# Decay rows of the first head pair: spread on chip by TensorE and ScalarE instead of loaded by DMA

## The chip, the cores and the metric

The kernel runs on one core of a Trainium2 chip. The metric is the device time of one execution in microseconds (us), the median of the runs shown. Engines are named as the profile names them: PE (TensorE), DVE (VectorE), ACT (ScalarE), POOL (GpSimd) and SP (SyncE, which here only issues DMAs).

## What is computed

Three stages follow one another: an attention with a decay, a mixture of experts with one expert for each token, and a dense feed-forward layer. Only the start of the attention matters here:

```
scores = scale * np.matmul(q, k.transpose(0, 1, 3, 2))
log_f = np.log(np.clip(f, 0.0001, 1.0))
cum = np.cumsum(log_f, axis=-1)
decay = cum[:, :, :, None] - cum[:, :, None, :]
scores = np.where(causal, -1000000000.0, scores + decay)
```

After this come a softmax over the last axis and the product with `v`. There are 4 x 8 = 32 heads, 576 positions and a head dimension of 64. The part of the decay that is constant along a row of the scores falls out of the softmax, so the kernel needs only one row of `cum` for each head, and the same row in every partition.

## The kernel before, in words

The function `attention` works on 16 pairs of heads. A pair has five blocks of query rows, u = 0 to 4, taken in the order 3, 0, 1, 4, 2. Block u < 4 covers 128 rows and 128(u+1) columns for each of the two heads; block 4 covers the last 64 rows of both heads at once and all 576 columns. The list `seq` holds the 80 (pair, block) steps and the loop from line 590 walks through them with lags: in one turn it computes the scores of a step, the softmax of the same step, and the transposes, products with v, normalisations and so on of earlier steps. Every engine takes its instructions in the order in which the program emits them; nothing is reordered by a scheduler. A helper tagged "T" owns three PSUM banks that are reused in turn: transposed q and k, the tails, the transposed probabilities and small results all pass through these three. Tag "s" gives three banks to the scores.

The decay goes as follows. `fs` (32 heads in 32 partitions, 576 columns) is loaded, clipped (L172), its logarithm taken (L174), summed up by a scan (L178) and multiplied by -8 (L179), which gives `cum`, again 32 x 576 in float32. The ScalarE queue stores it to the DRAM tile `ncum` (L564). `load(i, "c")` then fetches for pair i a tile `cb` of 128 x 3 x 576: `cb[:, 0]` and `cb[:, 1]` hold the row of head 0 and of head 1 in all partitions, `cb[:, 2]` holds head 0 in partitions 0 to 63 and head 1 in 64 to 127 (L162, L163; four DMAs for a pair, all on SP's queue). The softmax of blocks 0 to 3 reads at most 512 columns of `cb[:, h]` (L311); block 4 reads `cb[:, 2]` in two halves of 288 (L322). The result of L311 is the row maximum `mx`, which the exponential on ACT (L314) needs.

The start, before the loop, in emission order:

- SP: loads of q, k and v of pair 0 and q of pair 1 (L149, L150); then `cb` of pair 0, then k, v and `cb` of pair 1.
- PE: transposes of q and k of pair 0 (`prep(0, 0)`, `prep(0, 1)`, L212) and of their last 64 rows (`prep(0, 2)`, L228).
- ACT and DVE: the transposed values are split into a rounded part in type F32R (`hi`, ACT) and a remainder (`lo`, DVE, L219); a score is the sum of three products hi·hi, hi·lo and lo·hi (L289).
- ACT then squares v of pair 0 (L254), squares the expert embeddings (L577), loads a table, takes a square root (L578), and loads the first table again (L579).
- DVE converts a number of constants (L710 to L713).

In the first turn of the loop (step (0, 3)) PE computes the scores, ACT takes the exponentials of head 0, PE transposes q of pair 1 (`prep(1, 0)`), ACT copies them to `qraw` (L221), POOL splits `qraw` (L222, L223), and ACT takes the exponentials of head 1. At the end of that turn the second half of `scale(0)` runs (a small matmul `vb`, L259, bits of it on DVE, L261, factors on POOL, L264 to L270), and then `vprep(0)` scales and splits v on POOL (L245 to L247). The next turn brings `prep(1, 1)`, the same for k of pair 1 (L212, `kraw` L221, L222, L223), and two turns later POOL makes `vmb` (L256), which the matmul `vb` of pair 1 (L259) reads; behind that matmul PE has the tails of pair 1 (L228) and the first products with v (L412).

Of the kernel before, what the change touches and what calls it, by code (L numbers as in the profile page):

```python
# [9 lines left out]
F32 = mybir.dt.float32  # L10
# [5 lines left out]
ACTF = mybir.ActivationFunctionType  # L16
# [8 lines left out]
B, H, S, D = 4, 8, 576, 64  # L25
# [6 lines left out]
T = 5 * B  # L32
# [24 lines left out]
def body(ctx, tc, q, k, v, f, emb, tau, w1, w2, win, wout, out):  # L57
# [38 lines left out]
    with ExitStack() as acc:  # L96
        ps_s = attention(tc, g, acc, q, k, v, f, emb, tau, w1)
        g.home = ctx.enter_context(tc.tile_pool(name="home", bufs=16, reuse_waits="tile"))
        ring = ctx.enter_context(tc.tile_pool(name="ring", bufs=8, reuse_waits="tile"))

        def wtile(dt=F32R, n=1024):
            return (ring.tile([128, n], dt, name="wh", tag="wh"), ring.tile([128, n], dt, name="wl", tag="wl"))

        g.wtile = wtile
        g.w2a = w2[0]
        with ExitStack() as rtx:
            route(tc, g, rtx.enter_context(tc.tile_pool(name="r_p", bufs=1)), ps_s)
# [12 lines left out]
def attention(tc, g, acc, q, k, v, f, emb, tau, w1):  # L120
    nc = tc.nc
    ident, xd, ncum, nrm = g.ident, g.xd, g.ncum, g.nrm
    with ExitStack() as ctx:
        cst = ctx.enter_context(tc.tile_pool(name="a_cst", bufs=1))
        ld = ctx.enter_context(tc.tile_pool(name="a_ld", bufs=3))
# [4 lines left out]
        ps_t = acc.enter_context(tc.tile_pool(name="a_pt", bufs=3, space=PSUM))  # L130
# [13 lines left out]
        loaded = {}  # L144

        def rows_in(t, src, i):
            b, h0 = i // 4, 2 * (i % 4)
            for h in range(2):
                nc.sync.dma_start(t[:, 0:4, h], src[b, h0 + h, 0:512, :].rearrange("(k p) d -> p k d", p=128))  # L149
            nc.sync.dma_start(t[0:64, 4], src[b, h0:h0 + 2, 512:S, :].rearrange("h p d -> p h d"))  # L150
            return t

        def load(i, what):
            r = loaded.setdefault(i, {})
            for nm in what:
                if nm == "v":
                    r[nm] = rows_in(vbuf[i % 3], v, i)
                elif nm == "c":
                    bh = 2 * i
                    c = r[nm] = ld.tile([128, 3, S], F32, name="cb", tag="cb")  # L160
                    for h in range(2):
                        nc.sync.dma_start(c[:, h], ncum[bh + h:bh + h + 1, :].to_broadcast([128, S]))  # L162
                        nc.sync.dma_start(c[64 * h:64 * h + 64, 2], ncum[bh + h:bh + h + 1, :].to_broadcast([64, S]))  # L163
                else:
                    r[nm] = rows_in(ld.tile([128, 5, 2, D], F32, name=nm + "t", tag=nm + "t"), q if nm == "q" else k, i)

        load(0, "qkv")
        load(1, "q")

        zer = cst.tile([128, 128], F32, name="zer")  # L170
        nc.vector.memset(zer, 0.0)
        nc.vector.tensor_scalar(fs, fs, 1e-4, 1.0, op0=ALU.max, op1=ALU.min)  # L172
        lf = cst.tile([B * H, S], F32, name="lf")
        nc.scalar.activation(lf, fs, ACTF.Ln)  # L174
# [2 lines left out]
        cum = cst.tile([B * H, S], F32, name="cum")  # L177
# [23 lines left out]
        consts = route_consts(tc, g, cst)  # L201
        next(consts)
        split = {}

        def prep(i, part):
            r = loaded[i]
# [33 lines left out]
        def vprep(i):  # L240
            r = loaded[i]
            vf, vp = r["v"], vpart[i % 3]
            vs = qk.tile([128, 5, 2, D], F32, name="vs", tag="vs", bufs=1)
            v1, v2 = vp[:, :, :, 0:D], vp[:, :, :, D + 2:2 * D + 2]
            nc.gpsimd.tensor_scalar(vs, vf, vscale[i], 0.0, op0=ALU.mult, op1=ALU.add)  # L245
            nc.gpsimd.tensor_scalar(v1, vs, 1.0, 0.0, op0=ALU.mult, op1=ALU.add)
            nc.gpsimd.tensor_sub(v2, vs, v1)  # L247
            r["vp"] = vp
# [315 lines left out]
        nc.scalar.dma_start(ncum, cum)  # L564
        prep(0, 1)
        prep(0, 2)
        load(0, "c")
        load(1, "kvc")
        vs0 = scale(0)
        next(vs0)  # L570
# [19 lines left out]
        for n in range(n_all + Lg + 1):  # L590
# [38 lines left out]
            for x in (pt_, sf):  # L629
                for _ in x:  # L630
                    pass
            if n == 0:
                for _ in vs0:
                    pass
                vprep(0)
# [1079 lines left out]
```

## Time and profile before

| | us |
|---|---|
| median of 3 runs | 892.55 |
| lowest, highest | 892.10, 892.96 |
| the profiled execution, its own time | 891.38 |
| its span, first to last instruction | 889.6 |

| engine | busy us | share of the span |
|---|---|---|
| PE | 855.0 | 96% |
| DVE | 699.5 | 79% |
| ACT | 564.4 | 63% |
| POOL | 377.1 | 42% |

A timeline row gives the start, the duration, the engine, the line, the operation, what it writes and reads with its shape, a count where equal instructions are merged (then the duration is that of all of them), and in brackets the idle time of the engine before it with what ended that time. The end of a row is its start plus its duration. PE's ends are modelled. A wait that hung on several things is put down to the one that came last by the profile. Queue names end in q (SPq: SP issuing a DMA).

### The profile page before, as it was taken

Reading aid. Unit: us, or ns where it says so; the run is one execution under the profiler, and the core shown is the slowest. Engines: PE = TensorE matmul, PEld = TensorE weight load, DVE = VectorE, ACT = ScalarE, POOL = GpSimd, SP = SyncE. Lnnn points to the kernel's source line nnn. Section 1 sums busy time; section 2 is a strip of 40 time slices with the busy share of each in tenths; the row PEclk is TensorE's granted clock in tenths of the full one; section 3 lists DMA queues with packets and bytes.
Section 4 is the critical chain, followed back from the end, with each engine's and each line's share of the span. In section 5 each row is a group of like instructions: output and inputs, shape, how many; then the busy total and the mean of one; then the engine's idle time right before and its main releaser. Section 6 shows DMA issues by size and latency. Waiting matters only on the chain.

```text
span 889.6 us, 17326 instructions
## 1 busy us (share of the span) xinstructions
PE 855.0 (96%) x6308; PEld 594.8 (67%) x6308; DVE 699.5 (79%) x1542; ACT 564.4 (63%) x1052; POOL 377.1 (42%) x517
## 2 busy tenths in 40 slices
PE   5999999999759999999999999999999999999998
PEld 4788787887658999998889744444444445664443
DVE  4888888888879677787789778878878778777875
ACT  5778879788564566665856766655555444666453
POOL 6678677777142322422604233344223322435221
PEclk9999999999879999999999999999999999999999
DMA  7978566682336977878668110002000100100001
GB/s 173 195 162 170 136 153 157 143 235 58 109 113 244 319 281 271 273 261 287 229 222 299 37 50 13 25 13 72 25 1 36 37 1 1 60 1 25 1 1 47
DMA packets 102830, 109.73 MB, mean 123 GB/s; under 512 B 62964, under 2 KB 72200, under 8 KB 102736
## 3 DMA queue, kind: packets, MB, share of 16 engines
q1 hardware_dynamic: 97266, 93.49, 36.3%
q0 software_dynamic: 5184, 14.87, 4.7%
q8 instruction: 51, 0.84, 0.4%
q14 instruction: 43, 0.35, 0.1%
q10 hardware_dynamic: 286, 0.17, 0.1%
HBM read 93.31 MB, written 15.20 MB: 122 GB/s over the span
## 4 chain that ended last, share of the span: by engine, by line
PE 62%; DVE 5%; POOL 2%; issue 1%; ACT 1%; DMA 0%; DVEq 0%; POOLq 0%
PE h L1580 18%; PE y L1626 14%; PE y L1188 12%; PE h L1208 11%; PE t L1626 5%; POOL e L1594 1%; DVE r L1591 1%; DVE e L1605 1%; PE t L1110 1%; PE t L1441 1%; PE h L1278 1%; DVE wl L1057 1%; DVE e L1606 0%; DVE u L1593 0%; DMA xg<-xd,gidx 0%
## 5 line engine op out<-in xcount | busy, mean ns | idle before, releaser
L1594 POOL TENSOR_TENSOR e<-u,e 128x512 f32<-128x512 f32 (+1 forms) x80 | 105.0, 1313 | 238.8 <-DVE u L1593 235.5
L1590 ACT ACTIVATE e<-h,s_h 128x512 f32<-128x512 f32 (+1 forms) x80 | 51.2, 640 | 114.9 <-PE h L1580 114.9
L1626 PE MATMUL y<-dw,gh 128*128 128x512 f16 x448 | 113.6, 379 | 0.2 <-ACT ob L1634 0.2
L1612 DVE SCALAR_TENSOR_TENSOR gl<-e,s_gup,gh 128x512 f16<-128x512 f32 (+1 forms) x80 | 94.7, 1183 | 8.4 <-ACT gh L1610 7.9
L1626 PEld LDWEIGHTS <-gh 128*128 128x128 f16 x576 | 56.3, 98 | 64.8 <-issue 0.5
L340 DVE SCALAR_TENSOR_TENSOR pts<-pt,pts 128x512 f16<-128x512 f32 (+3 forms) x128 | 69.8, 567 | 12.8 <-ACT pts L337 12.0
L1208 PE MATMUL h<-xh,wh 128*128 128x384 f32 (+1 forms) x256 | 79.2, 309 | 0.6 <-DVE hl L1214 0.4
L1208 PE MATMUL h<-xl,wh 128*128 128x384 f32 (+1 forms) x256 | 79.0, 309 | 0.6 <-DVE xl L1112 0.6
L1591 DVE TENSOR_SCALAR r<-h,s_h 128x512 f32<-128x512 f32 (+1 forms) x80 | 55.6, 695 | 30.5 <-ACT e L1590 30.5
L1208 PE MATMUL h<-xh,wl 128*128 128x384 f32 (+1 forms) x256 | 78.8, 308 | 0.0
L1580 PEld LDWEIGHTS <-wh 128*128 128x128 f16 x480 | 46.9, 98 | 46.7 <-issue 0.3
L1580 PEld LDWEIGHTS <-wl 128*128 128x128 f16 x480 | 47.0, 98 | 46.4
L1610 ACT ACTIVATE gh<-e,s_gup 128x512 f16<-128x512 f32 (+1 forms) x80 | 53.7, 671 | 36.1 <-DVE e L1606 36.1
L337 ACT ACTIVATE pts<-pt 128x512 f16<-128x512 f32 (+3 forms) x128 | 58.5, 495 | 22.6 <-PE pt L360 11.0
L314 ACT ACTIVATE p<-sm,mx 128x512 f32<-128x512 f32 (+3 forms) x128 | 67.9, 558 | 1.7 <-DVE mx L311 1.5
L1188 PE MATMUL y<-wh,hh 128*128 128x512 f32 x168 | 67.7, 403 | 0.0
L1605 DVE TENSOR_TENSOR e<-r,e 128x512 f32<-128x512 f32 (+1 forms) x80 | 50.4, 630 | 21.3 <-POOL e L1594 21.3
L311 DVE CUSTOM_DVE_ANT_0 sm<-s,cb 128x512 f32<-128x512 f32 (+3 forms) x128 | 58.3, 484 | 11.0 <-PE s L291 6.5
L1188 PE MATMUL y<-wl,hh 128*128 128x512 f32 x168 | 65.7, 391 | 0.0
L1626 PE MATMUL y<-dw,gl 128*128 128x512 f16 x224 | 65.3, 379 | 0.0
L1580 PE MATMUL h<-yth,wh 128*128 128x512 f16 x192 | 64.9, 379 | 0.0
L1580 PE MATMUL h<-yth,wl 128*128 128x512 f16 x192 | 64.9, 379 | 0.0
(368 smaller groups left out, 2436.4 us busy)
## 6 DMA issues: line engine op xcount, KB each, us to landing
raw<-in_moe_w_dram SPq DMA_DIRECT2D x44, 512.0 KB, 4.9
spare<-in_moe_w_dram SPq DMA_DIRECT2D x24, 512.0 KB, 5.7
cb<-ncum SPq DMA_DIRECT2D x32, 288.0 KB, 4.9
raw<-in_moe_w_in_dram SPq DMA_DIRECT2D x16, 512.0 KB, 4.9
raw<-in_moe_w_out_dram SPq DMA_DIRECT2D x16, 512.0 KB, 4.5
yg<-yd SPq DMA_DIRECT2D x18, 264.0 KB, 2.7
cb<-ncum SPq DMA_DIRECT2D x32, 144.0 KB, 4.8
qt<-in_q_dram SPq DMA_DIRECT2D x32, 128.0 KB, 2.8
```

Of the source, the lines that this page charges most:

```text
L311: nc.vector.tensor_tensor_reduce(out=s[:, 0:n], in0=ps[h][:, 0:n], in1=c[:, h, 0:n], scale=-0.125, scalar=1e30, op0=ALU.add, op1=ALU.min, ...
L314: nc.scalar.activation(p[:, 0:n], s[:, 0:n], ACTF.Exp, scale=-1.0, bias=m)
L337: nc.scalar.activation(hi, ps, ACTF.Copy, scale=UP)
L340: nc.vector.scalar_tensor_tensor(lo, ps, UP, hi, op0=ALU.mult, op1=ALU.subtract)
L1188: nc.tensor.matmul(py[a], x[:, 128 * a:128 * a + 128], w[:, fb % 2], start=(fb == 0 and m == 0 and w is wh), stop=(fb == 7 and m == 1))
L1208: nc.tensor.matmul(pl, x[:, fs], y[:, c], start=(c == 0 and m == 0), stop=(c == 3 and m == 2))
L1580: nc.tensor.matmul(pl, w[:, fs], x[:, d], start=(d == 0 and m == 0), stop=(d == 3 and m == 2))
L1591: nc.vector.tensor_scalar(r, pl, back, 0.0, op0=ALU.mult, op1=ALU.max)
L1594: nc.gpsimd.tensor_sub(e, u, e)
L1605: nc.vector.tensor_sub(d, r, d)
L1612: nc.vector.scalar_tensor_tensor(gl, d, s, gh, op0=ALU.mult, op1=ALU.subtract)
L1626: nc.tensor.matmul(PO[c][a], x, w, start=(fb == 0 and m == 0 and w is wh), stop=(fb == FB - 1 and m == 1))
```

## The change

The three rows of `cb` of pair 0 are no longer loaded. Four columns of the identity are spread into `pickrow`, a 32 x 3 x 128 tile of zeros and ones in float32. `decay(j)` multiplies the picker j with 512 columns of `cum`, both float32, into a PSUM bank of tag "T", and ACT copies the bank into `cb[:, j]`. For j = 2 the remaining 64 columns follow as a second matmul and copy. `decay(0)` and `decay(1)` are emitted right after `prep(0, 2)`, ahead of the loads of k, v and `cb` of pair 1 and of `scale(0)`; `decay(2)` is emitted at the end of the first turn of the loop, ahead of the second half of `scale(0)`. All other pairs load 512 instead of 576 columns into `cb[:, 0]` and `cb[:, 1]`. `ncum` is still stored.

```
                     for h in range(2):
-                        nc.sync.dma_start(c[:, h], ncum[bh + h:bh + h + 1, :].to_broadcast([128, S]))
+                        nc.sync.dma_start(c[:, h, 0:512], ncum[bh + h:bh + h + 1, 0:512].to_broadcast([128, 512]))
                         nc.sync.dma_start(c[64 * h:64 * h + 64, 2], ncum[bh + h:bh + h + 1, :].to_broadcast([64, S]))
...
         nc.vector.memset(zer, 0.0)
+        pickrow = cst.tile([B * H, 3, 128], F32, name="pickrow")
+        for j, (x, y, h) in enumerate(((0, 128, 0), (0, 128, 1), (0, 64, 0), (64, 128, 1))):
+            nc.vector.tensor_copy(pickrow[:, min(j, 2), x:y], ident[0:B * H, h:h + 1].to_broadcast([B * H, y - x]))
...
+        def decay(j):
+            c = loaded[0]["c"]
+            for lo, hi in ((0, 512), (512, S)) if j == 2 else ((0, 512),):
+                t = ps_t.tile([128, 512], F32, name="dec", tag="T")
+                nc.tensor.matmul(t[:, 0:hi - lo], pickrow[:, j], cum[:, lo:hi], start=True, stop=True)
+                nc.scalar.activation(c[:, j, lo:hi], t[:, 0:hi - lo], ACTF.Copy)
...
         prep(0, 2)
-        load(0, "c")
+        loaded[0]["c"] = ld.tile([128, 3, S], F32, name="cb", tag="cb")
+        decay(0)
+        decay(1)
         load(1, "kvc")
         vs0 = scale(0)
...
             if n == 0:
+                decay(2)
                 for _ in vs0:
```

## Rows read from the trace of the kernel before

**Rows 1.** Busy time by stretch: engines PE, PEld, DVE, ACT, POOL, granted clock, DMA share, GB/s

```profile
0.00:20.00 20.00, 10.58 (x48) 7.19 (x49) 9.45 (x41) 10.73 (x19) 12.32 (x55) 1.00 0.74 171
40.00:60.00 20.00, 20.00 (x277) 16.66 (x275) 16.58 (x63) 17.08 (x40) 16.66 (x24) 1.00 0.71 160
```

**Rows 2.** Waits, first 20 us: who waited for whom, total us, times, longest

```profile
POOL qhi L222 <- ACT qraw L221: 4.8, 1, 4.8
...
DVE sm L311 <- DMA cb<-ncum: 3.6, 2, 2.1
```

**Rows 3.** Waits of PE from 40 to 240 us, the longest total

```profile
PE s L289 <- DVE mx L322: 1.4, 3, 0.5
```

**Rows 4.** Timeline of ACT

```profile
8.91 0.23 ACT L231 ACTIVATE khi<-tail 128x64 fp32r<-128x64 f32 x1 [0.99 <-DVE qlo L232]
9.05 0.74 ACT L254 ACTIVATE vs<-vb 128x640 f32<-128x640 f32 x1
...
12.02 1.28 ACT L579 ACT_TABLE_LOAD   x1
13.82 0.72 ACT L314 ACTIVATE p<-sm,mx 128x512 f32<-128x512 f32 x1 [0.51 <-DVE mx L311]
14.45 0.58 ACT L221 ACTIVATE qraw<-tps 128x512 f32<-128x512 f32 x1
15.97 1.01 ACT L314 ACTIVATE p<-sm,mx 128x512 f32<-128x512 f32 x2 [0.94 <-DVE mx L311]
18.02 0.60 ACT L221 ACTIVATE kraw<-tps 128x512 f32<-128x512 f32 x1 [1.04 <-PE tps L212]
...
23.52 0.23 ACT L231 ACTIVATE qhi<-tail 128x64 fp32r<-128x64 f32 x1
...
24.99 0.78 ACT L328 ACTIVATE p<-sm,mx 128x576 f32<-128x576 f32 x1 [0.73 <-DVE mx L322]
...
31.88 0.74 ACT L254 ACTIVATE vs<-vb 128x640 f32<-128x640 f32 x1 [0.86 <-DMA vb<-in_v_dram]
```

**Rows 5.** Timeline of POOL

```profile
15.11 0.62 POOL L222 TENSOR_SCALAR qhi<-qraw 128x512 fp32r<-128x512 f32 x1 [4.80 <-ACT qraw L221]
...
21.56 1.28 POOL L223 TENSOR_TENSOR klo<-kraw,khi 128x512 fp32r<-128x512 f32 x1
22.81 0.19 POOL L256 TENSOR_SCALAR vmb<-vm 128x1 bf16<-128x1 f32 x1
```

**Rows 6.** Timeline of PE

```profile
4.47 1.09 PE L212 MATMUL tps<-ident,qt 128*128 128x128 f32 x4 [4.47 <-DMA qt<-in_q_dram]
...
7.86 0.79 PE L289 MATMUL s<-khi,qhi 64*128 64x512 f32 x2 [0.28 <-ACT khi L218]
...
9.95 0.40 PE L291 MATMUL s<-maskb,identb 128*128 128x128 bf16 x2
...
16.90 1.09 PE L212 MATMUL tps<-ident,kt 128*128 128x128 f32 x4 [1.83 <-DMA kt<-in_k_dram]
...
22.29 0.44 PE L350 MATMUL pt<-ident,p 128*128 128x128 f32 x2
23.05 0.16 PE L259 MATMUL vb<-vmb,onesb 128*128 128x1 bf16 x1 [0.32 <-DMA qt<-in_q_dram]
```

**Rows 7.** Line 212 over the whole span: duration ns min/median/max, first and last start us

```profile
L212 PE MATMUL tps<-ident,qt x64: 272/273/447, 4.5 to 206.8; 128*128 128x128 f32 x64
```

**Rows 8.** The chain that ended last, one piece: start, us, what (F32R matmuls, 512 columns)

```profile
282.91 12.29 PE y L1188 x54
```

**Rows 9.** Timeline of DVE

```profile
3.56 0.47 DVE L172 TENSOR_SCALAR fs<-fs 32x576 f32<-32x576 f32 x1 [2.55 <-DMA fs<-in_f_dram]
...
7.45 0.69 DVE L219 TENSOR_TENSOR qlo<-tps,qhi 128x512 fp32r<-128x512 f32 x1
8.06 0.68 DVE L219 TENSOR_TENSOR klo<-tps,khi 128x512 fp32r<-128x512 f32 x1
...
13.09 0.69 DVE L311 CUSTOM_DVE_ANT_0 sm<-s,cb 128x512 f32<-128x512 f32 x1 [2.14 <-DMA cb<-ncum]
```

**Rows 10.** Timeline of SP's queue

```profile
8.97 0.35 SPq L162 DMA_DIRECT2D cb<-ncum  x1
...
11.03 1.14 SPq L149 DMA_DIRECT2D kt<-in_k_dram  x2
```

## The prediction

> **What bounds the kernel now.** I read the stretches first, then the waits, then each engine's timeline up to 35 us. From 40 us on PE is busy in all of a 20 us stretch, in the first 20 us in little over half [rows 1]; from 40 to 240 us the longest total wait of PE is 1.4 us, and it is for DVE [rows 3]. So this kernel is a start of some 23 us that fills slowly and then one long stretch that PE paces. The change acts on the start alone, and a shift of the moment at which PE gets going is carried to the end one for one.
>
> In the start DVE waits 3.6 us for `cb` of pair 0 [rows 2]. That is the wait that the change removes, and it looks like the bound. It is not: the first softmax step on DVE runs at 13.09 us [rows 9] and ACT's exponential follows at 13.82, but ACT has its own queue before it. It goes without a break from the square of v at 9.05 to the end of the second table load at 12.02 + 1.28 = 13.30 us [rows 4]. With `cb` there at once, the exponential could move from 13.82 to 13.30: the wait is worth 0.52 us at most.
>
> What ends last in the start is read backwards from PE's matmul `vb` of pair 1 at 23.05 [rows 6]. The profile names a DMA for that wait, but the matmul reads `vmb`, which POOL finishes at 22.81 + 0.19 = 23.00 [rows 5]. POOL has been at work since 15.11 with gaps of some tenths at most: it splits q of pair 1, makes the factors, scales and splits v, splits k (ends at 22.84), makes `vmb` [rows 5]. At 15.11 it had waited 4.80 us for `qraw`, which ACT ended at 14.45 + 0.58 = 15.03 behind that first exponential [rows 2, 4, 5]. Behind `vb` stand PE's tails of pair 1, then ACT at 23.52 and, through DVE, the exponential at 24.99 [rows 4]. So the chain is: ACT's queue to 13.30, exponential, `qraw`, POOL to 23.00, `vb`, all the rest. **Whatever is put into ACT's queue ahead of the first exponential, beyond those 0.52 us, is paid at the end.**
>
> **The change part by part.**
>
> Pickers on DVE: four copies of 32 partitions and up to 128 columns. No row has the shape; four times 0.47 (32 x 576, wider) makes 1.9 us at most, four times nothing at least. DVE idles 2.55 us before L172 [rows 9], so they cost nothing; without that cover they would delay `cum`, which is done well before its reader, PE at 8.19 (next).
>
> The two matmuls on PE. Their banks are the fourth and fifth of tag "T", which has three: the first takes over that of q and waits for DVE's qlo, to 7.45 + 0.69 = 8.14; the second that of k, to 8.06 + 0.68 = 8.74 [rows 9]. With 0.05 for the release (`vmb` to `vb` above) PE starts at 8.19. Before, it had started the scores at 7.86 [rows 6]; these now stand behind both matmuls.
>
> The length of such a matmul is not in the trace: no float32 product that isn't a transpose exists. Bounds from the nearest rows. Below, one pass of F32R: 12.29 / 54 = 0.228 us for 512 columns late in the kernel [rows 8]. [...] Between, the float32 transposes: four take 1.09 us and one takes 0.447, so each adds (1.09 - 0.447) / 3 = 0.214 for 128 columns [rows 6, 7], 0.86 for 512, two passes. Above, four passes: 4 x 0.43 = 1.71. I take **1.71**. [...] A modelled 0.23 (0.447 - 0.214) follows until the result is there. So the first runs from 8.19 and is there at 10.13, the second from 9.90, there at 11.84.
>
> [...]
>
> The two copies on ACT: 0.60 each, as `kraw` [rows 4]. They stand behind khi, which ends at 8.91 + 0.23 = 9.14, and ahead of the square of v. The second can start at 11.84 and ends at 12.44. Everything behind it shifts by 12.44 - 9.14 = 3.30, so ACT is through at 16.60 instead of 13.30, and the exponential goes from 13.82 to 16.60: **+2.78**. Its maximum is ready: the scores took 7.86 to 10.35 [rows 6], so from 11.61 they end by 14.1, and L311 takes 0.69. Queued behind ACT's wait are `qraw` (17.81) and with it POOL's row, `vmb` (25.78) and `vb` (25.83).
>
> With two passes the matmuls are there at 9.28 and 10.13, the second copy ends at 10.73, the shift is 1.59, the exponential +1.07. With one pass ACT takes the copies back to back, 9.14 to 10.3, and the exponential is +0.6 late.
>
> `decay(2)`: 512 and 64 columns, 1.9 us of PE and some 0.8 of ACT. PE has that time, waiting for `qraw` in any case: `vb` of pair 0 now gets the bank of q of pair 1. ACT's two copies come behind the second exponential, about 18.4 to 19.2. The transposes of k of pair 1 need the first copy's bank, so they go from 16.90 to about 19.0, 2.1 late; PE's work up to 22.73 [rows 6] then ends by 24.8, inside the wait for `vb` at 25.83. Nothing is added, by 1 us.
>
> Loads: SP's four issues from 8.97 to 11.03 go [rows 10], so k, v and `cb` of pair 1 are issued about 2.8 us earlier, and PE's wait of 1.83 for k at 16.90 [rows 6] vanishes. It lay beside POOL's chain; zero. The later wait of ACT for v at 31.88, 0.86 [rows 4], goes too; behind it ACT next waited for PE, so I count nothing. The 64 columns less per load: no PE wait in the long stretch is for a DMA worth naming; zero. On both I allow a gain of 0.5.
>
> The sum is +2.78 against the profiled 891.38, that is 894.2; the median of the runs lies 1.17 higher, so 892.55 + 2.78 = **895.3 us**.
>
> **The rivals.**
>
> Cheap matmuls (one or two passes). For it: the float32 transposes show two. Against: they multiply by a single one. 892.55 + 0.6 to 1.1 = 893.2 to 893.6: less than 0.2% (1.8 us), about what a measurement of this kernel can tell from no change.
>
> Faster, because the load was the bound after all. For it: DVE's 3.6 us [rows 2] and PE's 1.83 for k are real, and both go; 892.55 - 1.83 = 890.7. It decides only if ACT has finished both copies by 9.14 + 0.52 = 9.66, or if POOL's rows, whose spans are rough, are not the chain. Against: with one pass the second copy ends at 10.3, and `vb` started 0.05 after `vmb`.
>
> [...]
>
> **How the numbers follow.** The forecast has 0.59, cheap matmuls 0.20, the load as the bound 0.13, the clock 0.08. Slower by over 0.2% is forecast and clock, 0.67; within is cheap matmuls, 0.20; faster 0.13. The likeliest case's own range is 894.6 to 896.0. From 892.9 to 897.0 it holds the forecast, the cheap matmuls and half of the clock.
>
> **What would show it.** Right: ACT's copies near 10.1 and 11.8, a square of v near 12.4, the first exponential near 16.6 with no wait before it, `qraw` ending near 17.8, POOL without a gap from there to `vmb` near 25.8, `vb` 0.05 later, and later stretches as before. Wrong: matmuls under 1 us, an exponential before 15, POOL waiting between `qraw` and `vmb`, or a shift at `vb` that has shrunk or grown by 40 us.

## The result, and the profile after

The changed kernel takes 896.54 us (median of 7 executions, 896.12 to 900.78) beside 892.10 for the kernel before (median of 7, 890.85 to 892.96). The ratio of the mean times is 1.0059, 95% interval 1.0047 to 1.0072: 5.3 us slower, 4.2 to 6.4 (the medians differ by 4.4). The direction was forecast, and 896.54 lies below the upper end of the forecast, 897.0. But that end was 4.45 us above the 892.55 from which the forecast was counted, the forecast itself was 2.75 us, and the mean loss is about twice that. The executions also spread more: five of the seven took 896.1 to 896.7, one 897.8, one 900.78. The profiled execution is the longest of them, so its trace shows every loss at once. Repeats of the same kernel below tell which of them are always there.

| | before | after |
|---|---|---|
| profiled execution, us | 891.38 | 900.78 |
| its span, us | 889.6 | 899.0 |
| its mean granted clock | 0.988 | 0.981 |
| ACT's `qraw` of pair 1 starts | 14.45 | 17.49 |
| PE's `vb` of pair 1 starts | 23.05 | 26.11 |
| POOL scales v of pair 1 / of pair 2 | 25.75 / 39.72 | 28.95 / 47.51 |

First, ACT's timeline in the changed kernel, which answers to [rows 4] (start, busy us, engine, line, operation, count, and in brackets the idle time before it and what released it):

```profile
9.76 0.22 ACT L241 ACTIVATE khi<-tail 128x64 fp32r<-128x64 f32 x1 [0.77 <-DVE qlo L242]
10.41 0.60 ACT L213 ACTIVATE cb<-dec 128x512 f32<-128x512 f32 x1 [0.43 <-PE dec L212]
12.11 0.60 ACT L213 ACTIVATE cb<-dec 128x512 f32<-128x512 f32 x1 [1.11 <-PE dec L212]
12.61 0.73 ACT L264 ACTIVATE vs<-vb 128x640 f32<-128x640 f32 x1
...
15.56 1.28 ACT L591 ACT_TABLE_LOAD   x1
16.86 0.72 ACT L324 ACTIVATE p<-sm,mx 128x512 f32<-128x512 f32 x1
17.49 0.58 ACT L231 ACTIVATE qraw<-tps 128x512 f32<-128x512 f32 x1
...
36.75 0.74 ACT L264 ACTIVATE vs<-vb 128x640 f32<-128x640 f32 x1
```

ACT waits for each of PE's decay products, 0.43 and 1.11 us, and what stood behind khi runs behind the second copy: the square of v at 12.61 instead of 9.05, the exponential at 16.86 instead of 13.82, without a wait before it. The maximum that it needs had long been there: DVE's first softmax step starts at 14.03 now. The last line matters later: the square of v of pair 2 no longer waits for its load.

Next PE's timeline, which answers to [rows 6]:

```profile
8.30 3.78 PE L212 MATMUL dec<-cum,pickrow 32*128 32x512 f32 x4 [0.73 <-DVE qlo L229]
12.01 0.80 PE L299 MATMUL s<-khi,qhi 64*128 64x512 f32 x2
...
14.77 2.39 PE L212 MATMUL dec<-cum,pickrow 32*128 32x512 f32 x4
18.21 0.16 PE L269 MATMUL vb<-vmb,onesb 128*128 128x1 bf16 x1 [1.05 <-ACT qraw L231]
...
19.33 1.06 PE L222 MATMUL tps<-ident,kt 128*128 128x128 f32 x4
...
26.11 0.16 PE L269 MATMUL vb<-vmb,onesb 128*128 128x1 bf16 x1 [1.96 <-POOL vmb L266]
```

Each float32 matmul is two records in the trace. The two products for `decay(0)` and `decay(1)` are PE's from 8.30 to 11.87, if the modelled tail of the last record, 0.21, is taken off: 1.78 us each on average. The first took 1.87, the second 1.71, its two records being 0.86 us apart. The `vb` of pair 1 comes 3.06 us later than before. The k transposes come at 19.33 and PE's 1.83 us of waiting for k are gone, as foreseen.

What comes behind `vb` was not foreseen. PE's waits from 24 to 60 us in the changed kernel (who waited for whom, total us, times, longest):

```profile
PE av L422 <- DVE vbits L271: 2.1, 1, 2.1
PE vb L269 <- POOL vmb L266: 2.0, 1, 2.0
```

and the same wait in the kernel before, 23 to 56 us:

```profile
PE av L412 <- DVE vbits L261: 1.0, 1, 1.0
```

Stretches of the changed kernel, with the columns of [rows 1] (the granted clock stands before the DMA share):

```profile
24.00:28.00 4.00, 2.04 (x29) 1.63 (x27) 1.73 (x7) 1.94 (x7) 2.85 (x7) 0.76 1.27 192
28.00:32.00 4.00, 4.00 (x26) 3.01 (x24) 2.21 (x8) 2.19 (x4) 3.57 (x7) 0.50 0.35 72
...
40.00:44.00 4.00, 1.93 (x27) 1.80 (x24) 3.74 (x18) 1.77 (x4) 0.12 (x1) 0.89 0.00 0
44.00:48.00 4.00, 4.00 (x45) 3.13 (x44) 2.64 (x10) 1.61 (x4) 2.04 (x8) 0.68 0.48 126
```

Behind each of the two waits PE is busy all the time, but the granted clock is at 0.50, the lower level, from about 26 to 32.5 us and again from about 43 to 46.5. Before, every stretch from 20 to 44 us shows 1.00.

So there are three losses to tell apart: ACT's queue (+3.06 at `vb`), a longer wait of PE for `vbits` (2.1 instead of 1.0), and the granted clock behind PE's waits. DVE's timeline shows where the second comes from; `vbits` is one of its operations. In the changed kernel:

```profile
38.89 1.27 DVE L542 CAST w<-it 128x40 f32<-128x40 int32 x1
```

and in the kernel before:

```profile
33.05 0.18 DVE L532 CAST w<-it 128x40 f32<-128x40 int32 x1
33.14 0.18 DVE L533 CAST w8v<-it 128x40 f32<-128x40 int32 x1
```

These are `pick_consts`, two small constants for the routing that the kernel makes behind its gate weights. The first cast takes 1.27 us instead of 0.18. POOL's timeline says what lay beside it: first the changed kernel, then the one before.

```profile
37.67 0.38 POOL L266 TENSOR_SCALAR vmb<-vm 128x1 bf16<-128x1 f32 x1 [0.39 <-ACT vs L264]
...
38.84 1.27 POOL L233 TENSOR_TENSOR klo<-kraw,khi 128x512 fp32r<-128x512 f32 x1
```

```profile
32.80 0.19 POOL L256 TENSOR_SCALAR vmb<-vm 128x1 bf16<-128x1 f32 x1 [1.36 <-ACT vs L254]
...
33.98 1.26 POOL L223 TENSOR_TENSOR klo<-kraw,khi 128x512 fp32r<-128x512 f32 x1
```

After, the cast starts 0.05 us behind POOL's split of k of pair 2 and ends 0.05 us behind it. Before, both casts were through 0.66 us ahead of it (33.32 to 33.98); POOL had waited 1.36 us for ACT's square of v, and in the changed kernel that wait is 0.39. Why the cast takes longer beside the split is in no row; the times are, 1.27 and 0.18 us.

### The profile page after: what moved, and what is told of

The parts are those of the page before. It is cut to its first block, busy times and chain, and to the rows that moved or that the text cites. A ratio compares the mean times of both kernels' runs of the same rounds, so it can differ in the third digit from the quotient of the medians.

```text
span 899.0 us, 17342 instructions
## 1 busy us (share of the span) xinstructions
PE 864.8 (96%) x6316; PEld 600.6 (67%) x6316; DVE 700.9 (78%) x1546; ACT 566.4 (63%) x1056; POOL 376.9 (42%) x517
## 4 chain that ended last, share of the span: by engine, by line
PE 63%; DVE 3%; POOL 2%; issue 1%; ACT 1%; DMA 0%; DVEq 0%; POOLq 0%
PE h L1593 18%; PE y L1639 14%; PE h L1221 13%; PE y L1201 12%; PE t L1639 4%; POOL e L1607 1%; DVE r L1604 1%; DVE e L1618 1%; PE t L1123 1%; PE t L1454 1%; PE h L1291 1%; DVE e L1619 0%; DMA xg<-xd,gidx 0%; DVE u L1606 0%; POOL out_dram L1650 0%
```

## The experiments

All theories agree on the direction; the runs were chosen to price each loss. One mark serves throughout: when POOL scales v of pair 2. Little is added behind it: in the profiled executions pair 2 is at +7.79 us, pair 3 (53.02 to 61.40) and the last pair (217.27 to 225.65) both at +8.38.

**The changed kernel twice more**, on other chips, to see which of the three losses recur.

> The changed kernel once more. Theory 1 (ACT's queue): qraw starts near 17.5 us and vb of pair 1 near 26.1, 3.1 later than before. Theory 2 (two DVE casts, L542, caught beside POOL's split of k of pair 2): one cast takes 1.27 again instead of 0.18, so pair 2's L255 stands 4.2 to 4.5 us later than the 39.72 of before, if PE's clock stays at the upper level. Together 892.1 + 3.06 + 1.1 to 1.4 = 896.3 to 896.6. Rival (the loss is PE's clock): every execution shows two stretches at 0.50 after PE's waits at 24.2 and 40.2, and L255 of pair 2 stands at 47.5; without such stretches the time would be that of before plus 1 at most.

> The changed kernel as it is, on the same chip as the kernel with the late load of v. All theories: vb of pair 1 at 26.1, the cast 1.27 us long, 896.3 us where the clock stays up and up to 901 where it falls behind PE's waits; ratio 1.005 to 1.007.

Measured: 897.83 us, ratio 1.0064 (1.0041 to 1.0086), and 898.04 us, ratio 1.0072 (1.0058 to 1.0086). `vb` of pair 1 is at 26.10 and 26.12, and the cast falls on POOL's split both times. The granted clock differs. Stretches of the first repeat, then of the second:

```profile
24.00:28.00 4.00, 2.58 (x39) 1.89 (x38) 2.11 (x9) 2.22 (x7) 2.90 (x8) 1.00 1.24 196
28.00:32.00 4.00, 4.00 (x51) 3.39 (x49) 3.92 (x12) 3.81 (x8) 3.50 (x6) 1.00 0.59 122
...
40.00:44.00 4.00, 4.00 (x44) 3.35 (x42) 3.39 (x12) 1.58 (x5) 1.31 (x6) 0.60 0.25 74
```

```profile
24.00:28.00 4.00, 2.38 (x34) 1.92 (x34) 2.09 (x9) 2.26 (x8) 2.91 (x7) 0.84 1.25 204
28.00:32.00 4.00, 4.00 (x32) 3.03 (x33) 2.47 (x9) 2.38 (x4) 3.51 (x6) 0.74 0.50 104
...
40.00:44.00 4.00, 3.08 (x55) 2.72 (x56) 3.76 (x15) 1.52 (x5) 0.51 (x3) 1.00 0.00 0
```

The first fell to the lower level only behind its second wait and took 898.39 us, the second only behind `vb` (a wait of 1.62 us) and took 898.09; the execution profiled at the beginning fell at both places and took 900.78. All 17 executions of the changed kernel sort by their mean granted clock: eight at 0.987 took 896.1 to 897.3 us, six at 0.985 or 0.986 took 897.8 to 898.4, three at 0.981 took 900.5 to 900.8. The means of the three groups are 896.6, 898.1 and 900.7. So the queue and the cast recur, and the clock costs nothing, about 1.5 or about 4 us on top. That two places cost more than twice one goes with the rows: the lower level behind `vb` lasted from about 26 to 32.5 us in the first execution, from about 26.7 to 30.1 in the second repeat.

**The two copies by DVE**, so that ACT's queue is free of them.

```
-                nc.scalar.activation(c[:, j, lo:hi], t[:, 0:hi - lo], ACTF.Copy)
+                nc.vector.tensor_copy(c[:, j, lo:hi], t[:, 0:hi - lo])
```

> The copies of the decay rows on DVE instead of ACT, all else as changed. Theory 1: ACT goes from khi (9.98) straight to the square of v, is free near 14.2, and the first exponential now waits for DVE's maximum, near 14.9; vb of pair 1 near 24.1, 2 us earlier than in the changed kernel: 894.4 to 894.8. Rival (PE's added matmuls or its clock): PE does the same work in the same order, so 896.5.

Measured: 895.70 us, ratio 1.0039 (1.0027 to 1.0051). ACT:

```profile
15.01 0.72 ACT L324 ACTIVATE p<-sm,mx 128x512 f32<-128x512 f32 x1 [0.92 <-DVE mx L321]
15.63 0.58 ACT L231 ACTIVATE qraw<-tps 128x512 f32<-128x512 f32 x1
```

`qraw` comes 1.86 us earlier than in the changed kernel, `vb` only 1.15 earlier, at 24.96, where 2 us were expected. POOL now waits 0.67 us before `vmb`, for ACT's square of v, which stands behind work that waits for PE. PE's own queue is late: its transposes of k are at 18.84, still 1.94 later than before, behind the float32 products and a wait of 0.55 us for a copy that DVE now makes. Without ACT's share most of the loss stays, and what is left lies on PE's queue. The cast is 1.27 us long here too (34.94, beside POOL's split at 34.90), and no stretch from 20 to 48 us is below 1.00: POOL scales v of pair 1 at 27.66 and of pair 2 at 42.73, 15.07 apart. Before, they were 39.72 - 25.75 = 13.97 apart. The collision costs the difference, **1.10 us**.

**The product in F32R.** The picker and a second copy of the cumulated decay are F32R; this leaves out the low part of the decay.

```
-        pickrow = cst.tile([B * H, 3, 128], F32, name="pickrow")
+        pickrow = cst.tile([B * H, 3, 128], F32R, name="pickrow")
...
+        cumr = cst.tile([B * H, S], F32R, name="cumr")
+        nc.vector.tensor_scalar(cumr, cum, -8.0, None, op0=ALU.mult)
...
-                nc.tensor.matmul(t[:, 0:hi - lo], pickrow[:, j], cum[:, lo:hi], start=True, stop=True)
+                nc.tensor.matmul(t[:, 0:hi - lo], pickrow[:, j], cumr[:, lo:hi], start=True, stop=True)
```

> [...] Theory 1: the matmuls are there at about 8.9 and 9.4, ACT's second copy ends near 10.6 to 11.1, the first exponential stands near 15, qraw near 15.6, vb of pair 1 near 24.2: 894.3 to 894.9. If the length of the matmul does not matter (ACT's two copies alone are the cost): the same as the changed kernel less 0.3.

Measured: 895.48 us, ratio 1.0037 (1.0023 to 1.0051). The group of decay products here (duration in ns, shortest, median, longest) and in the changed kernel:

```profile
L214 PE MATMUL dec<-cumr,pickrow x4: 253/791/791, 9.0 to 14.0; 32*128 32x512 f32 x3, 32*128 32x64 f32 x1
```

```profile
L212 PE MATMUL dec<-cum,pickrow x8: 309/1056/1217, 8.3 to 16.7; 32*128 32x512 f32 x6, 32*128 32x64 f32 x2
```

One record for each matmul instead of two, 0.79 us with the modelled tail. The first exponential comes at 15.54 instead of 16.86 and `vb` at 24.76 instead of 26.11, 1.35 earlier. 1.9 were expected; the second copy of the decay is one more operation on DVE, and the first product starts at 9.05 instead of 8.30. The distance from pair 1 to pair 2 is 42.53 - 27.45 = 15.08: the cast once more, at the same 1.1 us.

**No second table load.** The square root among ACT's set-up work, which brings in a table and so a second load behind it [rows 4] (1.28 us each, at 14.05 and 15.56 us in the changed kernel), becomes a logarithm and an exponential.

```
-        nc.scalar.activation(en[:, 1:2], en[:, 0:1], ACTF.Sqrt)
-        nc.scalar.preload_act_table_set(LN_EXP)
+        nc.scalar.activation(en[:, 1:2], en[:, 0:1], ACTF.Ln)
+        nc.scalar.activation(en[:, 1:2], en[:, 1:2], ACTF.Exp, scale=0.5)
```

> The changed kernel with the square root as exp(0.5 ln x) on ACT, so that the two table loads behind the copies go; the copies stay on ACT. Theory 1: ACT is free near 13.9 instead of 16.84, the first exponential follows DVE's maximum near 14.75, qraw starts near 15.4 instead of 17.5; POOL no longer ends last, PE does, behind decay(2): transposes of k of pair 1 near 18.3, vb near 24.4 instead of 26.1: 894.5 to 895.5. Rival (the copies' wait for the matmuls is not what shifts qraw): vb stays at 26.1 and the time at 897.

Measured: 894.75 us, ratio 1.0033 (1.0021 to 1.0044). `qraw` is at 15.41, 2.08 earlier, and `vb` at 24.03, also 2.08 earlier, with nothing of the decay changed: ACT's queue sets `vb`, one for one, in the changed kernel. Neither table load is in this trace, which is 2.56 us; the rest is a new wait of 0.27 for DVE's maximum, and the two new activations.

**The two casts early**, first in the changed kernel, then in the kernel before. `pick_consts()` moves from behind the gate weights to a place ahead of the loop, where DVE has no POOL split beside it.

```
+        pick_consts()
         def ready(i, u):
...
-                pick_consts()
```

> The two casts of the pick constants and their memset (pick_consts) ahead of the loop, where DVE has time, instead of after step 6; all else as changed. Theory 2: vb of pair 1 stays at 26.1, the stretch between vb and L255 of pair 2 is 1.1 us shorter: 895.4. Rival (the cast's 1.27 lies beside other work): 896.5.

> Control for the casts: the kernel before with pick_consts moved ahead of the loop and nothing else. There the two casts take 0.18 each and meet no POOL split, so theory 2 expects at most the 0.36 us of the casts: 892.0 to 892.4, the same as before. Rival (the move itself is worth what the run with early casts gained): 891.0 to 891.3.

Measured: in the changed kernel 895.22 us, ratio 1.0033 (1.0020 to 1.0045), so some 2.6 us less than the changed kernel beside it on the same chip. In the kernel before 891.42 us, ratio 0.9992 (0.9982 to 1.0001): no difference that can be told from none. PE's waits from 24 to 60 us with the casts early:

```profile
PE vb L269 <- POOL vmb L266: 1.5, 1, 1.5
...
PE av L422 <- DVE vbits L271: 0.5, 1, 0.5
```

The second wait shrinks from 2.1 to 0.5 us, and 40 to 48 us show a clock of 1.00. The gain is more than the 1.1 us that I have put on the collision. Some 0.4 us of the rest is what the casts cost without any collision: in the kernel before, the same edit brings pairs 1 and 2 from 13.97 to 13.53 us apart. The wait for `vbits`, behind which the level fell to 0.50 in two of the three profiled executions of the changed kernel (waits of 2.1 and 2.0 us), has shrunk as well. In the kernel before the edit is worth no more than those 0.4 us, so the collision is not a price that both pay.

**The 512-column loads alone**, in the kernel before.

```
-                        nc.sync.dma_start(c[:, h], ncum[bh + h:bh + h + 1, :].to_broadcast([128, S]))
+                        nc.sync.dma_start(c[:, h, 0:512], ncum[bh + h:bh + h + 1, 0:512].to_broadcast([128, 512]))
```

> The kernel before with 512 instead of 576 columns in the two head rows of every pair, pair 0 too, and nothing else: the least part of the change alone. Every theory here: the start is not set by these bytes, and later no PE wait is for them: within 0.3 us of before, 891.7 to 892.3. A gain above 1 us would mean that the loads themselves paced something.

Measured: 892.10 us beside 892.02, ratio 1.0000 (0.9990 to 1.0010). This part of the change costs and gives nothing. Its profiled execution, 894.73 us, is the longest of ten: PE fell to the lower level behind a wait of 1.5 us before `vb` (0.62 from 24 to 28 us), DVE's casts came later, and the first met POOL's split (1.27 us). So both losses are within reach without the change; the change makes one of them, the cast, the rule.

**`decay(2)` left out**, its row loaded by two DMAs behind the loads of pair 1.

```
+        for h in range(2):
+            nc.sync.dma_start(loaded[0]["c"][64 * h:64 * h + 64, 2], ncum[h:h + 1, :].to_broadcast([64, S]))
...
-                decay(2)
```

> The changed kernel with the third row of pair 0 (the one that block 4 reads) loaded by two DMAs behind the loads of pair 1, and decay(2) left out. Theory 1: decay(2)'s 2.4 us on PE and 0.7 on ACT lie inside the wait for POOL's chain, vb of pair 1 stays within 0.2 of 26.1: the same as the changed kernel, 896.3 to 897.8. Rival (decay(2) is part of the loss): vb up to 0.7 earlier.

Measured: 899.20 us (898.31 to 900.48), ratio 1.0078 (1.0063 to 1.0093). PE:

```profile
26.14 0.16 PE L269 MATMUL vb<-vmb,onesb 128*128 128x1 bf16 x1 [5.64 <-POOL vmb L266]
```

and its stretches:

```profile
24.00:28.00 4.00, 1.86 (x27) 1.62 (x26) 0.87 (x4) 1.95 (x6) 2.85 (x7) 0.66 1.25 217
28.00:32.00 4.00, 4.00 (x27) 3.01 (x24) 2.24 (x8) 2.17 (x4) 3.57 (x7) 0.50 0.46 93
```

`vb` did not move (26.14 beside 26.11), so `decay(2)` cost nothing at `vb`. Yet with less work the kernel took at least 898.3 us in all four executions, at a mean granted clock of 0.981 to 0.983. PE now waits 5.64 us before `vb` instead of 1.4 to 2.0, and in the profiled execution the lower level, 0.50, follows. Of the changed kernel's 17 executions only three were at such a clock. That the longer wait is the reason in all four is read from their mean clock; the two loads that replace the product were not tried alone.

**PE kept busy ahead of `vb`.** The casts are early, and eight matmuls whose result nobody reads run ahead of `vb` of pair 1.

```
-            t = (at[i - 2, 0][:, VB:VB + 1] if i > 1 else ps_t.tile([128, 1], F32, name="vb", tag="T"))
+            t = (at[i - 2, 0][:, VB:VB + 1] if i > 1 else ps_t.tile([128, 512], F32, name="vb", tag="T"))
+            if i == 1:
+                kh = split[0]["k"][0]
+                spin(nc, t, kh[:, 0:128], kh[:, 0:512], 8)
+            t = t[:, 0:1]
```

> The changed kernel with early casts, and eight F32R matmuls of 512 columns into vb's bank ahead of vb of pair 1, whose results are overwritten; PE then works through most of its wait from 24.2 to 26.1. Theory 3 (what is lost beyond 3.06 + 1.1 comes from PE dropping to its lower level after such a wait): no stretch at 0.50 follows vb, and the executions spread less than with early casts alone (894.62 to 896.91), all near 894.6 to 895.2. Rival (the spread has another source): the same spread. If the level is still the lower one at 24, the eight take 3.6 us and vb stands up to 2 us later.

Measured: 895.52 us (895.05 to 896.30), ratio 1.0042 (1.0028 to 1.0056). The fillers lie in the gap and move nothing:

```profile
23.94 2.12 PE L117 MATMUL vb<-khi 128*128 128x512 f32 x8
26.14 0.16 PE L273 MATMUL vb<-vmb,onesb 128*128 128x1 bf16 x1
```

The stretches from 24 to 48 us show 1.00, where the kernel with early casts alone had 0.86 and 0.71 from 24 to 32 us in its profiled execution. The executions spread less, as expected (895.05 to 896.30 instead of 894.62 to 896.91), but they do not come down to the best of the early casts, two of the five are at a mean clock of 0.985 or 0.986, and the medians are the same (895.52 and 895.22). As a remedy it is inconclusive.

**v of pair 2 late again**, as it was before the change, to test whether the vanished wait for it brought the split onto the cast. First the load of v of pair 2 was issued behind k of pair 3, then behind the first decay row of pair 3.

```
-                load(now[0] + 2, "qkcv")
+                if now[0] == 0:
+                    load(2, "qkc")
+                elif now[0] == 1:
+                    load(3, "qk")
+                    load(2, "v")
+                    load(3, "cv")
+                else:
+                    load(now[0] + 2, "qkcv")
```

> The changed kernel, with the load of v of pair 2 issued behind k of pair 3 instead of ahead of q of pair 3, so that it is late again, as it was before the change. Theory (the vanished wait for v brought POOL's split of k of pair 2 forward onto DVE's cast): ACT's square of v of pair 2 waits again, by 0.5 to 2 us, POOL's split starts over 8 us behind its scaling of v of pair 1 instead of 7.25, the cast takes 0.18 us, PE's wait for vbits is 1.0 us or less, and the time is 1.1 us less than the changed kernel's best, 895.0 to 896.0. Rival (the change brings DVE's cast and POOL's split together in some other way, and the load does not matter): the cast takes 1.27 us again and the time is that of the changed kernel, 896.5 to 898. A third way: v is now so late that it sets POOL's next work itself, then the cast is free and the time 897 or more.

> The changed kernel with the load of v of pair 2 issued behind the first decay row of pair 3, at about 29.8 to 31.6 us, so that it lands near 35.5. Theory (the vanished wait for v brought POOL's split of k of pair 2 onto DVE's cast): ACT's square of v of pair 2 waits by 0.5 to 2 us, POOL's split starts 8 us or more behind its scaling of v of pair 1 instead of 7.25, the cast takes 0.18 us, PE's wait for vbits is about 1.0 us; time 895.0 to 896.0, more where the clock falls behind vb. Rival (they meet in some other way, whatever the load): ACT waits, the cast still takes 1.27 us, and the time is 896.5 to 898. A third way: v is so late that POOL's next work is late and PE waits for it, then the cast is free and the time 897 or more.

Measured: 896.75 us, ratio 1.0055 (1.0042 to 1.0068), and 896.13 us, ratio 1.0041 (1.0026 to 1.0056). The first missed its aim: the loads were issued at 26.5 to 29.2 us, v was there in time, and the cast was 1.27 us long. Its best execution, 895.43 at a mean clock of 0.990, is below all 17 of the changed kernel even so, and no trace says why. The second came to 894.7 and 894.9 in its best executions, also at 0.990; but two of its ten took 901 at 0.981, the profiled one among them, in which the lower level behind `vb` (0.50 from 28 to 32 us) made ACT itself late, so that v was no longer missed (its square of v of pair 2 starts at 36.85 without a wait), and the second cast took 1.25 us. By time alone neither run settles the question. A pair of kernels that should keep the level, by the eight fillers ahead of `vb`, followed: with v loaded later, and with v loaded early as in the change, the casts in their place in both.

> v of pair 2 loaded behind the first decay row of pair 3, and eight filler matmuls ahead of vb of pair 1, so that no stretch behind vb falls to the lower level. Theory (the vanished wait for v): ACT's square of v of pair 2 waits 0.5 to 2.5 us, POOL's split starts 8 us or more behind its scaling of v of pair 1 (28.8), both casts take 0.18 us, PE's wait for vbits is 1.0 us or less, POOL scales v of pair 2 some 14 us behind that of pair 1, and the time is 895.0 to 895.8. Rival (the load does not matter): the cast is 1.27 us long and the distance 15.1, as with the early load.

> The changed kernel with the same eight fillers ahead of vb of pair 1 and nothing else. Both theories: no low stretch behind vb, ACT does not wait for v of pair 2, POOL's split 7.25 us behind its scaling of v of pair 1, the cast 1.27 us, PE's wait for vbits 2.0 us, distance from pair 1 to pair 2 15.1 us where the level holds behind that wait and longer where it falls; time 896.3 to 898.

Measured: 895.60 us, ratio 1.0039 (1.0025 to 1.0053), with v late; 897.42 us, ratio 1.0060 (1.0043 to 1.0076), with v early. POOL and then DVE with v late:

```profile
29.27 0.80 POOL L255 TENSOR_SCALAR vs<-vb,vs 128x640 f32<-128x640 f32 x1
...
36.78 1.27 POOL L233 TENSOR_TENSOR klo<-kraw,khi 128x512 fp32r<-128x512 f32 x1
43.25 0.80 POOL L255 TENSOR_SCALAR vs<-vb,vs 128x640 f32<-128x640 f32 x1
```

```profile
36.57 0.18 DVE L546 CAST w<-it 128x40 f32<-128x40 int32 x1
36.66 0.18 DVE L547 CAST w8v<-it 128x40 f32<-128x40 int32 x1
```

and with v early:

```profile
29.50 0.80 POOL L255 TENSOR_SCALAR vs<-vb,vs 128x640 f32<-128x640 f32 x1
...
36.76 1.27 POOL L233 TENSOR_TENSOR klo<-kraw,khi 128x512 fp32r<-128x512 f32 x1
44.56 0.80 POOL L255 TENSOR_SCALAR vs<-vb,vs 128x640 f32<-128x640 f32 x1
```

```profile
36.80 1.27 DVE L546 CAST w<-it 128x40 f32<-128x40 int32 x1
```

All stretches from 20 to 56 us show 1.00 in both. In either kernel the cast starts 7.30 us behind POOL's scaling of v of pair 1. The split starts 7.51 behind it with v late, 7.26 with v early: the quarter of a microsecond that ACT waited for v was enough, though 0.5 us of waiting and a split at 8 us or more had been expected. (ACT's square of v began 0.55 us behind the start of the exponential ahead of it, instead of 0.29; the two semaphore rows of its line stand at 34.4 and 34.6 us, with v early both at 33.8.) With v late the casts are free, PE's wait for `vbits` is 1.0 instead of 2.1 us, and from pair 1 to pair 2 it is 13.98 us, as in the kernel before (13.97), instead of 15.06. The load's place alone makes that difference, 1.08 us. The medians are further apart, 1.8 us; two of the four executions with v early took 898 at a mean clock of 0.985.

**The start put in another order**, in the kernel before, from what the chain had shown: ACT's queue freed of both table loads, the third rows of `cb` loaded behind k, the casts early, and `qraw` ahead of the first exponential in the first turn.

```
-        load(0, "c")
-        load(1, "kvc")
+        c = loaded[0]["c"] = ld.tile([128, 3, S], F32, name="cb", tag="cb")
+        for h in range(2):
+            nc.sync.dma_start(c[:, h, 0:512], ncum[h:h + 1, 0:512].to_broadcast([128, 512]))
+        load(1, "k")
+        for h in range(2):
+            nc.sync.dma_start(c[64 * h:64 * h + 64, 2], ncum[h:h + 1, :].to_broadcast([64, S]))
+        load(1, "vc")
...
-        nc.scalar.activation(en[:, 1:2], en[:, 0:1], ACTF.Sqrt)
-        nc.scalar.preload_act_table_set(LN_EXP)
+        nc.scalar.activation(en[:, 1:2], en[:, 0:1], ACTF.Ln)
+        nc.scalar.activation(en[:, 1:2], en[:, 1:2], ACTF.Exp, scale=0.5)
...
+        pick_consts()
...
-            for c in "NSTXVPXLXGLFAL":
+            for c in "NSTXVPXLXGLFAL" if n else "NSTPXVXLXGLFAL":
...
-                pick_consts()
```

> A version from the reading of the start, built on the kernel before (the load stays): the square root on ACT as exp(0.5 ln x), so no table loads; qraw ahead of the first exponential on ACT; on SP the two 512-column rows, then k of pair 1, then the third row; casts early. Theory 1: ACT is free at 10.5 instead of 13.3, qraw stands near 11.3 instead of 14.45, POOL starts near 12, the transposes of k of pair 1 stand near 15.8 instead of 16.9 and are now the bound, vb of pair 1 near 21.8 instead of 23.05: 892.4 - 1.2 = 891.2. Rival (PE's start is set by the loads and its lower level alone): 892.4.

Measured: 890.40 us (median of 11, 889.82 to 891.50) beside 892.02, ratio 0.9983 (0.9974 to 0.9992). It is faster than both kernels. ACT and PE:

```profile
11.23 0.60 ACT L221 ACTIVATE qraw<-tps 128x512 f32<-128x512 f32 x1 [0.28 <-PE vb L259]
13.85 1.92 ACT L314 ACTIVATE p<-sm,mx 128x512 f32<-128x512 f32 x3 [2.02 <-DVE mx L311]
```

```profile
15.61 1.08 PE L212 MATMUL tps<-ident,kt 128*128 128x128 f32 x4 [0.51 <-DMA kt<-in_k_dram]
...
21.75 0.16 PE L259 MATMUL vb<-vmb,onesb 128*128 128x1 bf16 x1 [0.71 <-DMA qt<-in_q_dram]
```

and POOL:

```profile
21.50 0.19 POOL L256 TENSOR_SCALAR vmb<-vm 128x1 bf16<-128x1 f32 x1 [0.95 <-ACT vs L254]
```

The first exponential still waits for `cb` by DMA and is no earlier than in the kernel before (13.85 beside 13.82), and yet the kernel is faster: the wait for `cb` that the change removes did not bind. `qraw` is 3.22 us earlier, `vb` only 1.30. By now `qraw` does not set `vb`: POOL waits 0.95 us for ACT's square of v before `vmb`, and PE's transposes of k of pair 1, which wait for their load, moved by 1.29 (15.61 beside 16.90). From the start of that square (20.60 us) to `vmb` it is 0.90 us; in the kernel before the square starts at 21.89, so by the same 0.90 this chain would have brought `vmb` to 22.79, and POOL's own work brought it to 22.81. Two chains end together there, one through ACT's queue and POOL, one through the load of k and PE, and it took both to be relieved. The edits were made together, so their shares are not parted.

The mark, over all the profiled executions (shifts against the kernel before, in us; the last column is the profiled execution's time minus the median of the kernel before on that chip):

| kernel | `vb` pair 1 | v scaled, pair 2 | time |
|---|---|---|---|
| start in another order | -1.30 | -1.74 | -2.2 |
| kernel before, casts early | 0.01 | -0.44 | +0.4 |
| 512 columns alone | 0.13 | 2.67 | +2.7 |
| copies by DVE | 1.91 | 3.01 | +3.1 |
| product in F32R | 1.71 | 2.81 | +2.4 |
| no table loads | 0.98 | 2.86 | +4.0 |
| casts early | 3.04 | 4.03 | +3.8 |
| casts early, PE kept busy | 3.09 | 2.67 | +3.2 |
| v later, PE kept busy | 3.51 | 3.53 | +3.1 |
| v early, PE kept busy | 3.75 | 4.84 | +4.3 |
| changed kernel, again (two) | 3.05, 3.07 | 4.60, 5.61 | +6.0, +6.1 |
| v late | 3.05 | 5.52 | +5.7 |
| v later | 3.07 | 7.80 | +8.6 |
| `decay(2)` left out | 3.09 | 7.90 | +8.5 |
| changed kernel | 3.06 | 7.79 | +8.7 |

The shift at pair 2 gives the time to within 1.4 us in every row; the shift at `vb` doesn't, wherever a cast or a stretch at the lower level lies between.

## Why the prediction was wrong on the size

By its own steps:

- **The chain through ACT's queue** was right. `vb` moved by 3.06 us where 2.78 was worked out, POOL ran from `qraw` to `vmb`, and three edits that relieve ACT, PE or both moved `vb` back by 1.15 to 2.08. The 0.28 more is PE's: its first product began at 8.30 instead of 8.19 and took 1.87 us instead of 1.71; the second took 1.71.
- **1.71 us for a product**, and not 0.86, was the right choice. No run shows four passes, from which the 1.71 is made up; the runs show times. A product of 512 columns took 1.78 us on average (1.87 and 1.71) in two records, and 512 and 64 columns together took 2.39 us in float32 (from 14.77 us, changed kernel) and 0.84 us in F32R (from 13.44 us, product in F32R), a modelled tail in either. With 0.86 the exponential would have been put at +1.07 instead of +2.78.
- **`decay(2)` at nothing** was right on the path (26.14 without it, 26.11 with it). What was not seen is that it fills a gap: without it PE's wait before `vb` is 5.64 us, and all four executions took 898.3 us or more.
- **Pickers, 512 columns** at nothing: right for the second, 1.0000. The four copies of the pickers took 0.65 us in DVE's idle time, but DVE's scan that makes `cum` starts at 4.88 to 4.92 us in all the traces with pickers, at 4.78 to 4.80 in those without, and the remainder of q, behind which PE's first product starts, at 7.55 instead of 7.45. That is the 0.11 by which the product began late; why the scan is later is not shown.
- **The vanished wait of ACT for v, 0.86 us, was the step that failed.** It was counted at nothing, since "behind it ACT next waited for PE". That looked at ACT alone. POOL's `vmb` and its split of k stand behind that square too. With v there in time the split comes forward against DVE: without a low stretch between (copies by DVE, product in F32R) it starts 7.24 and 7.27 us behind POOL's scaling of v of pair 1, before the change 33.98 - 25.75 = 8.23. The cast keeps its 7.3 and is met. `vbits` comes late, and PE waits 2.1 us instead of 1.0: +1.10. The pair of kernels that differ only in the place of v's load shows the same, 1.08. The sum is then 3.06 + 1.10 = 4.2 us, or 892.1 + 4.2 = 896.3, where the eight executions at a mean clock of 0.987 took 896.1 to 897.3. The rest of the mean loss of 5.3 us is mostly the clock: the two of the seven executions at 0.985 and 0.981 raise the mean by 0.8.
- **The clock** was given 0.08, and half of that case stands in the range up to 897.0. No row of the kernel before shows a price for it; its stretches from 0 to 48 us all read 1.00. In the changed kernel it is a third loss, in nine of 17 executions, at some 1.5 us for one place and some 4 for both. The places are behind `vb` and behind the wait for `vbits`, where the granted clock fell to 0.50 in the execution profiled first. That executions without a profile lose it in the same places is read from their mean clock alone, and in other kernels the mean clock sorts the times less well (v later, PE kept busy: 895.14 at 0.986, 895.60 at 0.987).
- **The load as the bound** and **cheap matmuls** fell: the change gained nothing from PE's 1.83 us, and no product took under 1 us. The wait for k was close to binding all the same: with ACT's queue relieved it sets `vb`, as the start in another order shows.

Open: why a wait of PE is followed by the lower level in one execution and not in the next (before `vb`, 1.96 us was and 1.95 with v late was not); why the fillers ahead of an unchanged cast put `vb` at 26.80 instead of 26.11; and 1.0 us that the changed kernel's first profiled execution lost behind 225 us (+8.38 there, +9.4 in the span).

## What to carry to other kernels

A value that is moved from a DMA to compute is priced at the queue that has to carry it: here DVE waited for the load with time to spare, while the engine given the copies had none (`vb` came 3.06 us later). When a load becomes early, follow every engine that its wait had held back, and ask what now runs beside what; here two small casts had passed a long split on another engine by 0.66 us, and meeting it cost 1.10 us. And a wait of the bounding engine cost more here than its length where the clock fell to 0.50 behind it, some 1.5 us on top for one place and some 4 for both: the kernel that left work out ahead of such a wait took 899.20 us (ratio 1.0078, where the changed kernel had 1.0059 to 1.0072), though fillers put there on purpose gained nothing that could be told (895.52 beside 895.22).

## What was not expected of the hardware

- A cast of 128 x 40 numbers on DVE took 0.18 us in the kernel before, with no split beside it, and 1.27 us in the changed kernel, where it started 0.05 us behind POOL's subtraction of 128 x 512; it ended 0.05 us behind POOL.
- PE's granted clock fell behind waits of 1.6 and 1.96 us before `vb` in two executions of the changed kernel (0.74 and 0.50 from 28 to 32 us), and stayed at 1.00 behind 1.42 in the third. It fell behind 1.50 and 1.51 with 512 columns alone (0.62 from 24 to 28 us) and with the casts early (0.71 from 28 to 32 us), and stayed at 1.00 behind 1.95 with v late, so in these runs the length of the wait did not decide alone. Behind 5.64 us it fell (0.50 from 28 to 32 us), and that kernel, which has less to do, took 898.3 us or more in every execution.
- A product of two float32 matrices over 512 columns held PE for 1.78 us on average in the changed kernel (8.30 to 11.87 us), in two records; in F32R it made one record of 0.79 us with its tail. So early PE's work took about twice its later time in the kernel before, four float32 transposes 1.09 us from 4.47 us and eight 1.04 from 101.75, though the granted clock reads 1.00 in both places.
